# The last three units of a convolution kernel laid out in one list, with the products of points 0 and infinity of the last unit's parts ahead of the other sums

## The chip, the cores and the metric

The kernel runs on one core of one Trainium2 chip. The metric is the device time in microseconds. The core has five engines that work side by side, each on its own queue of instructions in order: PE (matmuls and transposes, results in PSUM), DVE (vector), ACT (activations and copies), POOL and SP. Transfers are issued by SP, ACT or POOL and carried out by 16 DMA engines. [...]

## The reference

A convolution of width 3 along the sequence, then a batch normalisation per output channel, then silu:

```python
B, S, C = 2, 2048, 1024        # bf16
K = 3; P = K // 2
xp = jnp.pad(x, ((0, 0), (P, P), (0, 0)))
y = sum(jnp.einsum('bsc,cd->bsd', xp[:, k:k + S, :], w[k]) for k in range(K))
inv_std = 1.0 / jnp.sqrt(var + 1e-5)
y = (y - mean) * (g * inv_std) + b
return _silu(y)
```

## The kernel before

The convolution is done in a transformed domain. Six neighbouring output rows (R = 6) come from eight products (NJ = 8), one for each of eight points: 0, plus and minus one, plus and minus two, plus and minus a half, and infinity. A batch of 2048 rows has NB = 342 such groups, the columns of all later tiles. First x is loaded in windows and transformed by small matmuls (line 258) into `T_sb`, bf16; ACT and DVE copy the results out of PSUM (lines 269 and 271). The weights of the points are formed as sums and differences, two points at a time (lines 175 and 192).

A unit is one block of 128 output channels of one batch: 8 blocks times 2 batches give 16 units. Each unit holds four PSUM banks, and the units take banks 0 to 3 and 4 to 7 in turn. A product (line 296) is eight matmuls that sum over the 1024 input channels. Products of plus and minus points share a bank: the plus product is copied out by ACT (`plus`, lines 307 and 309), the minus product is added on top, and DVE (`combine`, line 314) gets sum and difference from the two. So `minus_one` leaves a sum and a difference in the tile `sd`; `minus_two` makes the three tiles `t0`, `t1`, `t2`, each two outputs wide, from `sd` and the two low banks; `minus_half` makes from them and the two high banks the six outputs: rows 0 and 1 in the low banks, rows 4 and 5 in the high banks, rows 2 and 3 in `t1`. Only row 0 needs the product of point 0, and only row 5 that of infinity. These two are added on top of bank 0 and bank 3 last of all (`first` and `last`), and ACT applies scale, offset and silu (line 319) into `yT`: row 0 and row 5 by one instruction each, rows 1 and 4 by one, rows 2 and 3 by one.

In a unit's `run`, the finish of the unit before is woven in. A whole unit then goes out by a transposing transfer on SP (`turn`, line 427) and five stores (`store`, lines 438 and 442), on SP, or on POOL for the last three whole units.

I call the last units n, q, p and then the last one, which is worked as two parts: a, of 229 columns (SPLIT), in banks 4 to 7, and b, of 113 columns, in banks 0 to 3. The parts are turned by PE transposes instead (`flip`, line 399), copied out of PSUM by DVE (line 400) and stored in pieces (`ship`, lines 414 and 420). Lines 501 to 547 of the kernel before are a written order of calls: each call issues all its instructions at once, and so sets each engine's queue. Copies of a plus product live in `cpool`, three buffers; `dpool` and `ypool2` hold `sd` and the `t` tiles. Each part's products 0 and infinity come last on PE (lines 533, 535, 540, 542). Stores of part a: six on SP and POOL; of b: one on ACT and a small one on SP, after everything.

Of the kernel before, what the change touches and what calls it, by code (L numbers as in the profile page):

```python
# [9 lines left out]
ALU = mybir.AluOpType  # L10
FP32 = mybir.dt.float32
# [4 lines left out]
P = 128  # L16
R = 6
NJ = 8
# [4 lines left out]
XBUFS = 12  # L23
SPLIT = 229
WT = 21

@with_exitstack
def kernel(
# [10 lines left out]
    nc = tc.nc  # L39
# [3 lines left out]
    NB = -(-S // R)  # L43
    NT = B * NB
    NW = -(-NB // WT)
    LAST = NB - WT * (NW - 1)
    assert S % P == 0 and NB <= 512
# [7 lines left out]
    ypool = ctx.enter_context(tc.tile_pool(name="ypool", bufs=1))  # L55
    dpool = ctx.enter_context(tc.tile_pool(name="dpool", bufs=1))
    ypool2 = ctx.enter_context(tc.tile_pool(name="ypool2", bufs=2))
    cpool = ctx.enter_context(tc.tile_pool(name="cpool", bufs=3))
    opool = ctx.enter_context(tc.tile_pool(name="opool", bufs=2))
    xwin_scope = ExitStack()  # L60
    xpool = xwin_scope.enter_context(tc.tile_pool(name="xpool", bufs=XBUFS))
# [8 lines left out]
    rows = consts.tile([4 * DC, P], BF16, name="rows")  # L70
# [6 lines left out]
    def transform_matrix():  # L77
        v = nc.vector
        val = consts.tile([P, 3, WT], I32, name="val")
        nc.gpsimd.iota(val, pattern=[[1, 3], [-R, WT]], base=-1, channel_multiplier=1)  # L80
        m = consts.tile([P, 4, 3, WT], FP32, name="m")
        f = consts.tile([P, 3, 2, WT], FP32, name="f")
        c = consts.tile([P, 2, WT], FP32, name="c")
# [56 lines left out]
    def load_w(pair, k, half=None):  # L140
        if (pair, "tile") not in raw:
            raw[pair, "tile"] = wpools[pair % 2].tile([P, 3, CT, 2, P], BF16, name=f"wch{pair % 2}")
        wch = raw[pair, "tile"]
        h0, h1 = (0, 2) if half is None else (half, half + 1)
        cols = slice((2 * pair + h0) * P, (2 * pair + h1) * P)
        nc.sync.dma_start(  # L146
            out=wch[:, k, :, h0:h1].rearrange("p c h d -> p c (h d)"), in_=w_all[:, k, :, cols]
        )
        clock["dma"] += 1200.0 * (h1 - h0)
        for h in range(2):  # L150
            raw[2 * pair + h] = wch[:, :, :, h]
# [3 lines left out]
    def idle(work):  # L155
        if work:
            work.pop(0)()
# [122 lines left out]
    class Unit:  # L280
# [86 lines left out]
        def run(self, between, prev, finish, prepare=None):  # L367
# [19 lines left out]
            if prepare:  # L387
                idle(act_work)
                idle(dve_work)

        def flip(self, o, blocks, rows, bank, evac):
            i0, i1 = min(rows), max(rows)
            every = slice(i0, i1 + 1, 1 if i1 == i0 else (i1 - i0) // (len(rows) - 1))
            n = blocks[0][1]
            v = ps[:, bank].bitcast(BF16)[0:n, 0:len(rows) * len(blocks) * P]
            v = v.rearrange("p (i k d) -> p i k d", i=len(rows), k=len(blocks))
            for a, i in enumerate(rows):
                for q, (t, m, _) in enumerate(blocks):
                    nc.tensor.transpose(v[:, a, q], self.yT[:, i, t:t + m], ident)  # L399
            evac(o[0:n, every, blocks[0][2]:blocks[-1][2] + 1], v)  # L400

        def ship(self, o, block, lo, rows, queues):
            i0, i1 = min(rows), max(rows)
            every = slice(i0, i1 + 1, 1 if i1 == i0 else (i1 - i0) // (len(rows) - 1))
            outs = out[self.bi, :, self.dc * P:(self.dc + 1) * P]
            full = S // R
            t, m, k = block
            hi = min(t + m, full)
            cuts = [lo, lo + (hi - lo) // 16 * 16]
            if cuts[-1] < hi:  # L410
                cuts.append(hi)
            queues = list(queues)
            for c0, c1 in zip(cuts, cuts[1:]):
                queues.pop(0).dma_start(
                    out=outs[c0 * R:c1 * R].rearrange("(p i) d -> p i d", i=R)[:, every],
                    in_=o[c0 - t:c1 - t, every, k],
                )
            cut = [i for i in rows if i < S % R]
            if t + m > full and cut:
                queues.pop(0).dma_start(  # L420
                    out=outs[full * R + cut[0]:full * R + cut[-1] + 1].rearrange("(p i) d -> p i d", p=1),
                    in_=o[full - t:full - t + 1, cut[0]:cut[-1] + 1, k],
                )
# [57 lines left out]
    between = Between()  # L481
    seq = [(dc, bi) for dc in range(DC) for bi in range(B)]
    before = prev = None
    for i, (dc, bi) in enumerate(seq[:-1]):
        unit = Unit(dc, bi, i % 2 * 4)
        unit.run(between, prev, prev, 1 if i == 0 else 2 if i == 2 else dc + 2 if bi == 1 and 0 < dc < DC - 2 else None)
        if i == 0:
            while between.jobs:
                between()
            xwin_scope.close()  # L490
            olast = ctx.enter_context(tc.tile_pool(name="olast", bufs=1))
            wpools[1] = ctx.enter_context(tc.tile_pool(name="wpool1", bufs=1))
        if i in (0, 4, 8):
            for k in range(3):
                load_w(i // 4 + 1, k)
        if prev:
            prev.turn()
        if before:
            before.store([nc.gpsimd] * 5 if i == len(seq) - 2 else ())
        before, prev = prev, unit  # L500
    dc, bi = seq[-1]
    yT = olast.tile([P, R, NBP], BF16, name="yTlast")
    a, b = Unit(dc, bi, 4, 0, SPLIT, yT), Unit(dc, bi, 0, SPLIT, NB, yT)
    sp, ac, po = nc.sync, nc.scalar, nc.gpsimd
    rows = tuple(range(R))
    ablocks, bblocks = [(0, P, 0), (SPLIT - P, P, 1)], [(SPLIT, NB - SPLIT, 0)]
    free = (DC // 2) % 2
    turned = wpools[free].tile([P, 3, CT, 2, P], BF16, name=f"wch{free}").rearrange("p k c h d -> p (k c h) d")
    op, oa, ob = (
        turned[:, R * lo:R * hi].rearrange("p (i k) d -> p i k d", i=R)  # L510
        for lo, hi in ((0, NK), (NK, NK + 2), (NK + 2, NK + 3))
    )
    dve, act = nc.vector.tensor_copy, nc.scalar.copy
    a.scratch()
    b.scratch(a)
    a.plus(3, 1, between)
    a.plus(0, 3, between, 4.0)
    prev.silu_inner()
    prev.first(between)
    prev.last(between)  # L520
    a.minus_one(between)
    prev.turn(op)
    a.minus_two(between)
    before.store([po] * 5)
    prev.store([po] * 5)
    b.plus(3, 1, between)
    b.plus(0, 3, between, 4.0)
    a.plus(2, 5, between)
    b.minus_one(between)
    a.minus_half(between)  # L530
    b.minus_two(between)
    b.plus(2, 5, between)
    a.first(between)
    a.silu_inner()
    a.last(between)
    b.minus_half(between)
    a.flip(oa, ablocks, rows[1:5], 6, dve)
    a.ship(oa, ablocks[0], 0, rows[1:5], (sp,))
    a.ship(oa, ablocks[1], P, rows[1:5], (sp, po))
    b.first(between)  # L540
    b.silu_inner()
    b.last(between)
    a.flip(oa, ablocks, (0, R - 1), 5, dve)
    a.ship(oa, ablocks[0], 0, (0, R - 1), (sp,))
    a.ship(oa, ablocks[1], P, (0, R - 1), (sp, po))
    b.flip(ob, bblocks, rows, 1, dve)
    b.ship(ob, bblocks[0], SPLIT, rows, (ac, sp))

_INS = ['x', 'w', 'mean', 'var', 'g', 'b']
_OUTS = [((2, 2048, 1024), 'bfloat16')]  # L550
# [24 lines left out]
```

## Time and profile before

| what | value |
|---|---|
| median of 6 runs | 193.39 us (193.13 to 194.15) |
| profiled execution | 194.28 us |
| its span | 192.5 us |
| PE busy | 176.5 us, 92% of the span |
| DVE busy | 156.2 us, 81% |
| POOL busy | 148.5 us, 77% |
| ACT busy | 110.0 us, 57% |
| DMA | 32.30 MB, mean 168 GB/s |

The times of the runs and the profile are from different executions; the profiled one lies above the median, and its own time is 1.78 us more than its span. Start times are microseconds from the span's start. "SPq", "ACTq" and "POOL ... DMA_DIRECT2D" rows are issues of transfers, not the transfers themselves. A row of the timeline may merge several instructions ("x4"), and its brackets give the idle time of the engine before it and what ended that. A wait is put down to whatever came last.

### The profile page before, as it was taken

The numbers are of one execution on the slowest core, as the hardware profiler recorded it, in microseconds if no ns is written. First come the engines' busy times: TensorE is split into PE (matmuls) and PEld (weight loads), VectorE is DVE, ScalarE is ACT, GpSimd is POOL, SyncE is SP. The second block draws the span as 40 slices with busy tenths as digits, with TensorE's granted clock in tenths as the row PEclk, the third lists the DMA queues.
The fourth block names the chain that finished last, engine by engine and source line by source line (L and its number), as shares of the span: only waits on it lengthen the run. The fifth ranks groups of instructions, "written<-read, shape, count | busy, mean of one in ns | idle before, by whom it ended". The sixth has DMA issues, their size and how long they took to land.

```text
span 192.5 us, 3675 instructions
## 1 busy us (share of the span) xinstructions
PE 176.5 (92%) x1379; PEld 124.4 (65%) x1379; DVE 156.2 (81%) x220; ACT 110.0 (57%) x185; POOL 148.5 (77%) x93
## 2 busy tenths in 40 slices
PE   1857989999999999999999999999999999999860
PEld 1846768666666666666666666666666666678740
DVE  5668976689978799987998899879988998573860
ACT  3768886774546565465545563646283736367450
POOL 5559999906796879999999999699999780251780
PEclk9999999999999999999999999999999999999995
DMA  6999999074142837498759658959578294979973
GB/s 184 315 329 323 325 338 282 12 215 117 31 91 49 183 69 167 143 217 204 138 119 208 113 120 221 211 132 204 110 154 169 62 147 90 210 148 150 188 152 71
DMA packets 83567, 32.30 MB, mean 168 GB/s; under 512 B 69764, under 2 KB 79005, under 8 KB 83549
## 3 DMA queue, kind: packets, MB, share of 16 engines
q1 hardware_dynamic: 82012, 30.30, 69.4%
q0 software_dynamic: 784, 1.58, 3.9%
q10 hardware_dynamic: 752, 0.18, 0.5%
q8 instruction: 11, 0.18, 0.4%
q14 instruction: 8, 0.06, 0.1%
HBM read 14.82 MB, written 8.39 MB: 121 GB/s over the span
## 4 chain that ended last, share of the span: by engine, by line
PE 80%; DMA 7%; ACT 4%; SPq 3%; DVE 2%; issue 1%; ACTq 0%; DVEq 0%
PE ps L296 76%; DMA xw<-in_x_dram 4%; PE ps L258 3%; DMA xfirst<-in_x_dram 3%; ACT T_sb L269 3%; SPq L131 2%; ACT yTlast L319 2%; DVE T_sb L271 1%; SPq L146 1%; PE ps L399 1%; DVE ps L314 1%; DVE wch_2123 L400 0%; ACT pc L307 0%; ACTq L307 0%; DVEq L400 0%
## 5 line engine op out<-in xcount | busy, mean ns | idle before, releaser
L307 ACT COPY pc<-ps 128x342 f32<-128x342 f32 (+2 forms) x34 | 14.5, 427 | 33.0 <-PE ps L296 30.5
L258 PE MATMUL ps<-rm,xw 128*128 128x168 bf16 (+1 forms) x256 | 25.2, 241 | 8.0 <-DVE rm L101 3.9
L269 ACT CAST T_sb<-ps 128x672 bf16<-128x672 f32 (+1 forms) x37 | 25.6, 736 | 8.1 <-PE ps L258 7.9
L271 DVE CAST T_sb<-ps 128x672 bf16<-128x672 f32 x29 | 23.6, 855 | 7.8 <-PE ps L258 7.5
L258 PEld LDWEIGHTS <-xw 128*128 128x128 bf16 (+1 forms) x256 | 19.9, 100 | 13.2 <-DMA xw<-in_x_dram 7.6
L314 DVE SCALAR_TENSOR_TENSOR ps<-ps,pc 128x342 f32<-128x342 f32 (+2 forms) x34 | 16.9, 498 | 7.1 <-PE ps L296 5.5
L319 ACT ACTIVATE yT_142<-ps,beta,scale 128x342 bf16<-128x342 f32 (+1 forms) x24 | 17.4, 732 | 5.9 <-PE ps L296 5.9
L319 ACT ACTIVATE yT_143<-ps,beta,scale 128x342 bf16<-128x342 f32 (+1 forms) x21 | 15.4, 732 | 5.9 <-PE ps L296 5.9
L314 DVE SCALAR_TENSOR_TENSOR sd<-pc,ps 128x342 f32<-128x342 f32 (+2 forms) x17 | 8.3, 488 | 12.8 <-ACT sd L307 12.6
L438 POOL DMA_DIRECT2D out_dram<-o x8 | 6.1, 896 | 15.9 <-DMA o<-yT_142 9.2
L307 ACT COPY sd<-ps 128x342 f32<-128x342 f32 (+2 forms) x17 | 7.3, 429 | 9.9 <-PE ps L296 9.8
L309 ACT ACTIVATE pc<-ps 128x342 f32<-128x342 f32 (+2 forms) x17 | 7.5, 441 | 9.4 <-PE ps L296 6.6
L296 PE MATMUL ps<-T_sb,wch_1507 128*128 128x342 bf16 (+2 forms) x80 | 10.8, 279 | 0.5 <-DVE ps L314 0.4
L296 PE MATMUL ps<-T_sb,wch_156 128*128 128x342 bf16 x64 | 10.6, 307 | 0.0
L296 PE MATMUL ps<-T_sb,wch_678 128*128 128x342 bf16 x64 | 10.6, 307 | 0.0
L296 PE MATMUL ps<-T_sb,wch_1089 128*128 128x342 bf16 x64 | 10.6, 307 | 0.0
L296 PEld LDWEIGHTS <-wch_1507 128*128 128x128 bf16 x80 | 7.2, 97 | 3.2 <-issue 0.9
L192 POOL TENSOR_TENSOR u_668<-e_666,w1x_664 128x1024 bf16<-128x1024 f32 x2 | 4.2, 2128 | 6.5 <-DVE e_666 L175 6.5
L296 PEld LDWEIGHTS <-wch_678 128*128 128x128 bf16 x64 | 6.2, 97 | 3.1
L296 PEld LDWEIGHTS <-wch_156 128*128 128x128 bf16 x64 | 6.2, 97 | 3.1
L296 PEld LDWEIGHTS <-wch_1089 128*128 128x128 bf16 x64 | 6.2, 97 | 3.1
L296 PE MATMUL ps<-T_sb,u_292 128*128 128x342 bf16 x32 | 6.1, 308 | 0.1
(256 smaller groups left out, 494.2 us busy)
## 6 DMA issues: line engine op xcount, KB each, us to landing
xw<-in_x_dram SPq DMA_DIRECT2D x30, 256.0 KB
out_dram<-o SPq DMA_DIRECT2D x24, 192.0 KB
wch_156<-in_w_dram SPq DMA_DIRECT2D x6, 256.0 KB
wch_678<-in_w_dram SPq DMA_DIRECT2D x3, 512.0 KB
wch_1089<-in_w_dram SPq DMA_DIRECT2D x3, 512.0 KB
wch_1507<-in_w_dram SPq DMA_DIRECT2D x3, 512.0 KB
out_dram<-o SPq DMA_DIRECT2D x12, 120.0 KB
out_dram<-o POOLq DMA_DIRECT2D x4, 192.0 KB, 4.1
```

What stands on the lines that cost most here:

```text
L131: nc.sync.dma_start(out=xw[0:hi - lo, :], in_=x[bi, lo:hi, :])
L146: nc.sync.dma_start(out=wch[:, k, :, h0:h1].rearrange("p c h d -> p c (h d)"), in_=w_all[:, k, :, cols])
L192: nc.gpsimd.tensor_tensor(u[:, i], sums[dc, q], o, op=op)
L258: nc.tensor.matmul(v[:, c * nb // nct, c % (nct // nb)], lhsT=xw[0:rows, (c0 + c) * P:(c0 + c + 1) * P], rhs=rm[0:rows, :, 0:n], start=Tru ...
L269: nc.scalar.copy(dst, src)
L271: nc.vector.tensor_copy(dst, src)
L296: nc.tensor.matmul(self.bank[q], lhsT=lhsT, rhs=T_sb[:, ct, j, nsl], start=not add and ct == 0, stop=ct == CT - 1, skip_group_check=add,)
L307: nc.scalar.copy(dst, self.bank[q])
L309: nc.scalar.mul(dst, self.bank[q], by)
L314: nc.vector.scalar_tensor_tensor(out=out, in0=in0, scalar=scalar, in1=in1, op0=ALU.mult, op1=op1)
L319: nc.scalar.activation(self.yT[:, rows, self.lo:self.hi], src, ACT.Silu, bias=beta[:, dc:dc + 1], scale=scale[:, dc:dc + 1])
L438: q.dma_start(out=rows[lo * R:hi * R].rearrange("(p i) d -> p i d", i=R), in_=o[p0:p0 + hi - lo, :, k])
```

## The change

Five things change.

1. The loop over units stops one earlier, and unit p joins a and b in a list of steps, `ORDER`. A name in the list is a unit's letter (q, p, a, b) and a step: `1`, `2`, `3` the plus products, `n1`, `n2`, `n3` the minus products, a number with `c` its copy, with `d` its DVE combination, `t0` to `t2`, `y0` to `y2` the sums, `0` and `8` the products of point 0 and infinity, `s..` the silus, `T` and `S` turn and store, `f` and `S` with a number flip and ship.
2. For a and b, the product of point 0 is added on the bank of the one-points after their sum was copied out, and copied out again (`0c`); the product of infinity goes into bank 1 and is added by DVE to the difference of the one-points (`8d`). A new tile `z` holds the four values. `t0` and `t2` then read pairs of `z`, so that rows 0 and 5 have their extra products before the sums. Each part needs three silus of two rows each.
3. For q and p the arithmetic is as before; q's product of point 0 comes right after p's first product, and a's first, second and infinity products ahead of p's last two.
4. Part a is flipped in rows 4 and 5 (bank 6, copied by ACT) and rows 0 to 3 (bank 4, copied by DVE); part b in three pairs of rows, copied by DVE. Stores of a: SP, ACT and one on POOL for its last five groups; of b: both on SP.
5. `cpool` has four buffers.

```diff
+EVAC_A = [0, 1]
+SHIP_A = [[0, 0], [0, 1]]
+SHIP_B = [0, 0]
+EVAC_B = [0, 0, 0]
+ORDER = """
+p1 q0 p2 p1c pn1 qs1 p2c pn2 pn2d qs0 p3 pn1c q8 p3c pn3 pn1d nS a2 qs2 pt2 pt1 pt0 qs5 pn3d py0 py1 a1 py2
+a1c ps2 a8 ps1 p0 p8 a2c an1 qT an2 an1d b8 ps0 ps5 qS a8d b1 b1c an2d an1c a3 a0 bn1 at2 a3c an3 b3 at1 bn1d
+a0c bn1c b2 b2c at0 b3c b0 b0c an3d b8d bn2 ay0 ay1 ay2 as0 as2 bn2d bn3 bn3d bt0 as1 bt1 af1 by1 bt2 by0 pT
+bs1 bs0 by2 af0 bf0 aS1 bf1 bs2 pS aS2 aS0 bf2 bS
+"""
-    cpool = ctx.enter_context(tc.tile_pool(name="cpool", bufs=3))
+    cpool = ctx.enter_context(tc.tile_pool(name="cpool", bufs=4))
+        def steps(self, z):
+            s0, s1, d1, z5 = (z[:, q, self.lo:self.hi] for q in range(4))
+            pairs = {
+                "t0": (0, -0.0125, z[:, 0:3:2, self.lo:self.hi]), "t1": (1, -0.05, z[:, 1:3, self.lo:self.hi]),
+                "t2": (2, -0.2, z[:, 1:4:2, self.lo:self.hi]),
+            }
...
+            else:
+                f["n1c"] = lambda: self.copy(3, dst=s1)
+                f["n1d"] = lambda: self.combine(d1, self.pc[3], 2.0, self.bank[3], ALU.subtract)
+                f["0"], f["0c"] = part(3, 0, True), lambda: self.copy(3, dst=s0)
+                f["8"], f["8d"] = part(1, NJ - 1, False), lambda: self.combine(z5, self.bank[1], 1.0, d1)
+                for k, (key, (_, a, pair)) in enumerate(pairs.items()):
+                    f[key] = lambda k=k, a=a, pair=pair: self.combine(t(k), self.low, a, pair)
+                f["s0"] = lambda: self.silu(slice(0, 2), self.low)
+                f["s1"] = lambda: self.silu(slice(2, 4), self.y23)
+                f["s2"] = lambda: self.silu(slice(4, 6), self.high)
+            return f
...
-    for i, (dc, bi) in enumerate(seq[:-1]):
+    for i, (dc, bi) in enumerate(seq[:-2]):
...
+    z = olast.tile([P, 4, NB], FP32, name="z")
...
-    a.plus(3, 1, between)
-    a.plus(0, 3, between, 4.0)
-    prev.silu_inner()
-    prev.first(between)
-    prev.last(between)
...
+    steps = {}
+    for name, u in (("q", prev), ("p", p), ("a", a), ("b", b)):
+        steps.update((name + k, f) for k, f in u.steps(z).items())
+    steps["qT"] = prev.turn
+    steps["pT"] = lambda: p.turn(op)
+    steps["nS"] = lambda: before.store([po] * 5)
+    steps["qS"] = lambda: prev.store([po] * 5)
+    steps["pS"] = lambda: p.store([po] * 5)
+    queue = (sp, ac, po)
+    low, high = tuple(range(4)), (4, 5)
+    steps["af0"] = lambda: a.flip(oa, ablocks, low, 4, (dve, act)[EVAC_A[0]])
+    steps["af1"] = lambda: a.flip(oa, ablocks, high, 6, (dve, act)[EVAC_A[1]])
+    steps["aS0"] = ships_a(low, [queue[q] for q in SHIP_A[0]])
+    steps["aS1"] = ships_a(high, [queue[q] for q in SHIP_A[1]])
+    steps["aS2"] = lambda: a.ship(oa, ablocks[1], P + 96, low + high, (po,))
+    for q in range(3):
+        steps[f"bf{q}"] = flips(b, ob, bblocks, 2 * q, q, (dve, act)[EVAC_B[q]])
+    steps["bS"] = lambda: b.ship(ob, bblocks[0], SPLIT, tuple(range(R)), [queue[q] for q in SHIP_B])
+    for k in ORDER.split():
+        steps[k]()
```

More of the change, by code (lines that the diff above doesn't have):

```diff
@@ L389, in run, with old @@
                 idle(dve_work)
+        def steps(self, z):
[4 more added lines that the diff above has]
+            }
+            nop = lambda: None
+            put = lambda q, by=None: self.pc.__setitem__(q, self.copy(q, by=by))
+            part = lambda q, j, add: (lambda: self.product(q, j, add, nop))
+            t = lambda k: (self.t0, self.t1, self.t2)[k]
+            def old():
+                self.combine(self.sd[:, 1], self.pc[3], 2.0, self.bank[3], ALU.subtract)
+            late = self.hi - self.lo == NB
+            f = {
+                "1": part(3, 1, False), "1c": lambda: put(3), "2": part(0, 3, False), "2c": lambda: put(0, 4.0),
+                "n1": part(3, 2, True), "n2": part(0, 4, True), "3": part(2, 5, False), "3c": lambda: put(2),
+                "n3": part(2, 6, True),
+                "n2d": lambda: self.combine(self.bank[1], self.bank[0], -2.0, self.pc[0]),
+                "n3d": lambda: self.combine(self.bank[3], self.bank[2], -0.5, self.pc[2]),
+                "y0": lambda: self.combine(self.low, self.high, -1.6, self.t0),
+                "y1": lambda: self.combine(self.t1, self.high, -0.4, self.t1),
+                "y2": lambda: self.combine(self.high, self.high, -0.1, self.t2),
+            }
+            if late:
+                f["n1c"] = lambda: self.copy(3, dst=self.sd[:, 0])
+                f["n1d"] = old
+                for k, a in enumerate((-0.0125, -0.05, -0.2)):
+                    f[f"t{k}"] = lambda k=k, a=a: self.combine(t(k), self.low, a, self.sd)
+                f["0"], f["8"] = part(0, 0, True), part(3, NJ - 1, True)
+                f["s0"] = lambda: self.silu(0, self.bank[0])
+                f["s5"] = lambda: self.silu(R - 1, self.bank[3])
+                f["s1"] = lambda: self.silu(slice(1, 5, 3), self.mid)
+                f["s2"] = lambda: self.silu(slice(2, 4), self.y23)
+            else:
[9 more added lines that the diff above has]
+            return f
@@ L400, in flip, with ship @@
             evac(o[0:n, every, blocks[0][2]:blocks[-1][2] + 1], v)
-        def ship(self, o, block, lo, rows, queues):
+        def ship(self, o, block, lo, rows, queues, whole=False):
             i0, i1 = min(rows), max(rows)
@@ L408, in ship @@
             hi = min(t + m, full)
-            cuts = [lo, lo + (hi - lo) // 16 * 16]
-            if cuts[-1] < hi:
+            cuts = [lo, lo + (hi - lo) // 16 * 16] if hi - lo > 16 else [lo]
+            if cuts[-1] < hi and not whole:
                 cuts.append(hi)
@@ L498 @@
         if before:
-            before.store([nc.gpsimd] * 5 if i == len(seq) - 2 else ())
+            before.store()
         before, prev = prev, unit
-    dc, bi = seq[-1]
     yT = olast.tile([P, R, NBP], BF16, name="yTlast")
-    a, b = Unit(dc, bi, 4, 0, SPLIT, yT), Unit(dc, bi, 0, SPLIT, NB, yT)
+    z = olast.tile([P, 4, NB], FP32, name="z")
     sp, ac, po = nc.sync, nc.scalar, nc.gpsimd
-    rows = tuple(range(R))
-    ablocks, bblocks = [(0, P, 0), (SPLIT - P, P, 1)], [(SPLIT, NB - SPLIT, 0)]
     free = (DC // 2) % 2
@@ L512 @@
     )
-    dve, act = nc.vector.tensor_copy, nc.scalar.copy
+    ablocks, bblocks = [(0, P, 0), (SPLIT - P, P, 1)], [(SPLIT, NB - SPLIT, 0)]
+    p = Unit(*seq[-2], len(seq) % 2 * 4)
+    a, b = (Unit(*seq[-1], b0, lo, hi, yT) for b0, lo, hi in ((4, 0, SPLIT), (0, SPLIT, NB)))
+    p.scratch()
     a.scratch()
     b.scratch(a)
-    a.plus(3, 1, between)
-    a.plus(0, 3, between, 4.0)
-    prev.silu_inner()
-    prev.first(between)
-    prev.last(between)
-    a.minus_one(between)
-    prev.turn(op)
@@ L523 @@
[L523 to L547, printed above, removed]
+    def flips(u, o, blocks, i, bank, evac):
+        return lambda: u.flip(o, blocks, (i, i + 1), bank, evac)
+    def ships_a(rows, queues):
+        def go():
+            a.ship(oa, ablocks[0], 0, rows, queues[:1])
+            a.ship(oa, ablocks[1], P, rows, queues[1:2], True)
+        return go
@@ new lines @@
+    dve, act = nc.vector.tensor_copy, nc.scalar.copy
+    steps = {}
[9 more added lines that the diff above has]
+    steps["af0"] = lambda: a.flip(oa, ablocks, low, 4, (dve, act)[EVAC_A[0]])
```

## The prediction, made before the result was known

> **What bounds the kernel now.** I began with the whole-span view (PE busy 92%, DVE 81%, POOL 77%, ACT 57%), then took the chain that ended last, because shares alone do not say where the tail is set. Columns: start, duration, what.
>
> ```profile
> 40.74 137.37 PE ps L296 x968
> 178.19 0.36 ACT pc L307
> 178.59 0.96 PE ps L296 x8
> 179.57 0.42 DVE ps L314
> 180.71 0.97 PE ps L296 x8
> 181.70 1.84 ACT yTlast L319 x3
> 183.58 0.51 PE ps L399 x6
> 186.01 0.61 PE ps L399 x4
> 186.71 0.56 DVE wch_2123 L400
> ```
>
> From 40.7 to 178.1 us the matmuls run without a break, so nothing before 178 can pay unless it removes matmuls. After that PE, ACT and DVE hand the last unit to each other. The timeline of the tail gives the engines' queues (start, duration, engine, line, idle in brackets):
>
> ```profile
> 171.63 3.67 SPq L427 DMA_TRANSPOSE o<-yT_143  x1
> 175.82 2.86 SPq L427 DMA_TRANSPOSE wch_2123<-yT_142  x1
> 176.19 0.39 DVE L314 SCALAR_TENSOR_TENSOR sd<-pc,ps 128x229 f32<-128x229 f32 x1 [3.33 <-ACT sd L307]
> 182.15 2.93 POOL L438 DMA_DIRECT2D out_dram<-wch_2123  x4 [1.13 <-DMA wch_2123<-yT_142]
> 184.17 0.39 DVE L314 SCALAR_TENSOR_TENSOR ps<-ps,t_2126 128x226 f32<-128x226 f32 x1
> 185.18 2.04 SPq L414 DMA_DIRECT2D out_dram<-wch_2123  x4
> 187.30 0.69 ACTq L414 DMA_DIRECT2D out_dram<-wch_2123  x1
> ```
>
> The last matmul ends at 185.2 (start 184.02 plus 1.17), the last store is issued at 187.30, and the span ends at 192.5. The view of busy time by window says what happens in those 5.2 us (the last two columns are the DMA engines' share and GB/s):
>
> ```profile
> 188.00:188.25 0.25, 0.00 (x0) 0.00 (x0) 0.00 (x0) 0.00 (x0) 0.00 (x0) 0.50 0.92 197
> 188.50:188.75 0.25, 0.00 (x0) 0.00 (x0) 0.00 (x0) 0.00 (x0) 0.00 (x0) 0.50 0.11 22
> 189.00:189.25 0.25, 0.00 (x0) 0.00 (x0) 0.00 (x0) 0.00 (x0) 0.00 (x0) 0.50 0.88 191
> 190.50:190.75 0.25, 0.00 (x0) 0.00 (x0) 0.00 (x0) 0.00 (x0) 0.00 (x0) 0.50 0.06 12
> 190.75:191.00 0.25, 0.00 (x0) 0.00 (x0) 0.00 (x0) 0.00 (x0) 0.00 (x0) 0.50 0.00 0
> ```
>
> Part a's stores keep the DMA engines busy until 188.6; the last store (part b, 168 KB) moves from 189.0, 1.7 us after its issue, has stragglers to 190.75, and 1.75 us of closing follow. So two chains end nearly together: the compute chain to the last store's issue, and the DMA backlog of p's store (packets from 183.5), a's and b's.
>
> [...]one backlog, 85 to 100% busy from 183.5 to 188.5. [...]by 180.0 the hardware queue's bulk (both transposes) was over, yet POOL waited for p's transpose until 182.15 while q's store moved. [...]Here SP's 185.18 issue showed packets about 1.1 us later and ACT's 187.30 issue 1.7 us later[...]. The trace has 0.275 us for 113 columns and 0.40 for 229, about 0.15 fixed.
>
> **The change, step by step.** [...]Prices, all from rows after 150 us: a product holds PE 1.16, 0.79 or 0.40 us (342, 229, 113 columns), readable 1.32, 0.95, 0.57 after its start. The vector combine's starts are 0.545 us apart at 458 columns, 0.305 at 226; singles last 0.40 (229) and 0.275 (113), the next may start 0.085 earlier. ACT copies last 0.45, 0.355, 0.26 and overlap the next by 0.11; silus of 458 columns follow 0.63 to 0.66 apart, of 226 about 0.46. A hand-over costs 0.04.
>
> *Removed and added.* Per part one silu goes (0.54 or 0.44) and one ACT copy comes (0.355 or 0.26), plus one vector add (0.40 or 0.275). Matmuls and transposes are as many as before; PSUM evacuations go from 3 to 5 and part stores from 8 to 7. A fourth copy buffer only loosens ACT waits beneath the unbroken PE stretch: zero, since matmuls cover it. Before p nothing else moves.
>
> *PE.* The part products 0 and infinity leave the tail, so PE should no longer stop at 178 to 181: the same products back to back end at 182.9 instead of 185.2. That is 2.3 us won on PE. But the two infinity products now run ahead of b's first product: before, that started at 176.34; after, 176.34 + 0.79 + 0.40 - 0.09 (a's second product had waited 0.09 for q's silu, no longer) = 177.43. p's last product needs p's low and high sums from DVE; p's four-product's subtraction slips two products, its last sum comes at about 173.95 and the product at 174.29: 0.3 to spare.
>
> *Where the gain goes first.* ACT's queue has b's first copy ahead of a's copy after its minus-one product. b's product is readable at 177.43 + 0.57 = 178.00; its copy starts 178.04, a's 178.19, done 178.54. Vector's three a-sums queue behind that: they start 178.58, where they started 176.98 before. Vector is idle for nearly 1 us ahead of them.
>
> *The vector chain.* From 178.58: two sums to 179.67; b's difference waits for its product (start 179.42, readable 179.98), 180.02; third sum 180.21; a's half-difference 180.81 (product readable 180.77); b's infinity add 181.13; a's three results 181.32, 181.86, 182.41, the last readable 183.04; b's two differences 182.95, 183.14; b's six sums at 183.33, 183.64, 184.07 (a dependence), 184.37, 184.80 (another), 185.11; readable 185.50. Before it was 184.17 + 0.39 = 184.56. Vector is 0.94 later, although PE is 2.3 earlier.
>
> *The ACT chain.* a's high silu waits for 183.04: 183.08. Then a's inner silu 183.71, the copy of four transposes 184.37 (moved here from DVE; 512 columns, not shown on ACT: 0.59 by the slope of the three copies), b's silus 184.85 and 185.31, then ACT itself issues a store of a at 185.73, and the last silu is queued behind it. The issue costs 0.41 (SP's shortest such row) to 0.69 (ACT's row); at nothing, if ACT could run on, the silu starts 185.73. I take 0.5: 186.2, readable 186.75; two transposes 187.07; copy of 256 columns 0.29 (slope of the 512, 768 and 1024 rows): 187.40; last store issued 187.43. The same reckoning over the old order gives 187.08 where the trace has 187.30, so I add 0.22: 187.65, against 187.30. The compute chain is 0.35 later; with the bounds of the issue and the copy, -0.15 to +0.6.
>
> *Queues.* POOL stores q when its transpose has landed. q's transpose is issued at about 170.6 instead of 171.63 (q's last silu moved up), p's at 176.4 instead of 175.82 (p's last product is later by one part product). p's transpose lands about 0.6 later, so p's store starts near 182.75 and its packets near 184.1 instead of 183.5. POOL is queued there, with the 5-row piece of a behind it: one DMA now, so about as late as before. SP's queue holds four of a's and b's stores; the last store, now on SP, queues behind a's 224 KB. By bytes, a's packets then end at about 188.6 + 0.5 = 189.1 where before they ended 188.6 with 0.4 us idle after. b's packets start at the later of 189.1 and 187.65 + 1.1 to 1.7 = 188.75 to 189.35: about 189.3 against 189.0. The small second store behind it is hidden by the stragglers.
>
> **Sum.** +0.3 us: span 192.8. That execution took 194.28, 1.78 beyond its span and 0.89 over the median of six, 193.39; the difference is put on the median: **193.7 us**. This kernel's runs scatter by about half a percent, and 0.3% (0.58 us) is about what a measurement can tell from no change.
>
> **Rivals.** (1) Likeliest, 0.42: the chains cancel within 0.58 us as above; its own range is 192.9 to 193.95. (2) Slower by a collision, 0.22. Place: the DMA engines between 176 and 184. Before, q's store packets followed p's transpose; after, q's store is issued up to 1 us earlier and p's transpose 0.6 later, so they overlap[...]. It decides once p's transpose lands after about 183.2 (I expect 182.7): then a and b wait behind p one for one. One microsecond gives 193.7 + 0.9 = 194.6. For it: the 2.2 us between p's data and its landing before. Against: the bytes are unchanged. (3) Slower by the ACT queue, 0.16. Place: ACT from 183 to 187, where every delay moves the last silu one for one. With the issue at 0.69 and the 512-column copy at the 0.736 of the 672-column cast it is +0.3; it decides when the last silu starts after about 186.7 (0.22 included), and a further 0.3 of waits gives 194.3. For it: ACT has no idle left there in my reckoning. Against: none of its waits is on PE. (4) Faster, 0.20: ACT's issue holds nothing up (-0.45), and the last store has SP's 1.1 us delay instead of ACT's 1.7 (-0.6), provided that a's packets are gone by 188.3: the end is 0.75 earlier than my sum, 192.9, and 192.6 if the 512-column copy also hides. It decides once the last store's packets start before 188.4. For it: PE frees 2.3 us. Against: DMA share near 0.9 until 188.5. A change that never reaches the tail is excluded: the order on PE differs.
>
> **Range.** The low end holds rival 4 whole, 192.5; the high end rivals 2 and 3 with a collision of up to 1.4 us, 195.0. About 1 in 10 is left out on each side.
>
> **What would show it.** Right: matmuls unbroken to about 182.9 with the PE gap of 1 us now ahead of the first transpose; DVE idle about 0.9 us near 177.7, released by ACT; a's sums starting near 178.6; the last vector sum ending near 185.7; an ACT store issue ahead of the last silu; the last store issued near 187.65. Wrong: PE gaps before 182, p's transpose landing at or before 182.1 with the last store before 187.1 (faster), or after 183.2 with DMA still saturated at 190 (slower).

## The result

The change made the kernel slower: 196.58 us (median of 10 runs, 194.23 to 198.05) against 193.79 us (20 runs). The ratio is 1.0113, with a 95% interval of 1.0082 to 1.0145; ratios here are of fast runs alone, and two of these ten, at 197.87 and 198.05 us, count as slow, so the medians lie further apart than the ratio. I had predicted 193.7 us, within 0.3% of no change, as the likeliest, with 195.0 at the top of the range. The profiled execution took 195.84 us; its span is 194.1 us, 1.6 us more than before.

In this execution p's first product starts at 161.79 us, where it was 161.48, because the loading of x at the start took a little longer: in the chain, the load of `xfirst` ends at 20.65 us, before at 20.40, and PE's unbroken stretch starts at 41.04, before at 40.74. This offset of 0.31 us has nothing to do with the change: over the executions below, that start lies anywhere between 161.01 and 162.74 us. First the chain that ended last, of the changed kernel:

```profile
41.04 141.26 PE ps L306 x1024
182.31 0.47 PE ps L306 x7
182.78 0.56 DVE ps L324
...
186.92 0.85 POOL out_dram L495
188.28 0.56 POOL out_dram L471
```

The unbroken stretch of PE now reaches the last matmuls, so that part of the change works: PE no longer stops between 178 and 181. But the chain passes to POOL at 186.92, which it did not before. The timeline of the changed kernel shows what came late (start, duration, engine, line):

```profile
176.77 2.77 SPq L484 DMA_TRANSPOSE wch_2029<-yT_142  x1
177.09 2.95 POOL L495 DMA_DIRECT2D out_dram<-o  x4 [5.88 <-DMA o<-yT_143]
178.89 0.63 DVE L324 SCALAR_TENSOR_TENSOR t_2036<-ps,z 128x458 f32<-128x458 f32 x1 [0.71 <-ACT z L317]
184.84 2.93 POOL L495 DMA_DIRECT2D out_dram<-wch_2029  x4 [4.29 <-DMA wch_2029<-yT_142]
185.26 4.83 SPq L471 DMA_DIRECT2D out_dram<-wch_2029  x4
185.36 0.39 DVE L324 SCALAR_TENSOR_TENSOR ps<-ps,t_2036 128x226 f32<-128x226 f32 x1
185.55 0.36 ACTq L471 DMA_DIRECT2D out_dram<-wch_2029  x1
185.61 0.96 ACT L329 ACTIVATE yTlast<-ps,beta,scale 128x226 bf16<-128x226 f32 x2
186.62 0.72 DVE L457 COPY wch_2029<-ps 113x256 bf16<-113x256 bf16 x3 [0.27 <-PE ps L456]
190.13 0.64 SPq L477 DMA_DIRECT2D out_dram<-wch_2029  x1
```

The computing ends where it did: b's last copy is over at 186.62 + 0.72 = 187.34 (before 186.71 + 0.56 = 187.27), and 0.24 us earlier than before once the offset of 0.31 is taken off. The transfers are late. POOL waited until 184.84 for p's transpose, where it had been 182.15; the transpose, issued at 176.77, took 8.1 us instead of 6.3. Beside it runs q's store on POOL, issued 0.32 us after the transpose. In the kernel before it came 1.72 us after it:

```profile
177.54 2.96 POOL L438 DMA_DIRECT2D out_dram<-o  x4 [6.62 <-DMA o<-yT_143]
```

And SP's four stores (now three of a and the large one of b) stretch over 4.83 us of issues and end at 190.09, although b's data were ready at 187.34. Before, SP's four stores, all of a, took 2.04 us.

The windows of the changed kernel (last two columns: DMA share and GB/s) show a hole, then a backlog:

```profile
184.00:185.00 1.00, 0.80 (x12) 0.64 (x12) 0.97 (x3) 1.00 (x3) 0.16 (x1) 1.00 0.01 3
185.00:186.00 1.00, 0.21 (x4) 0.04 (x1) 0.97 (x4) 1.00 (x3) 1.00 (x2) 1.00 0.06 16
188.00:189.00 1.00, 0.00 (x0) 0.00 (x0) 0.00 (x0) 0.00 (x0) 0.85 (x2) 0.50 1.12 198
191.00:192.00 1.00, 0.00 (x0) 0.00 (x0) 0.00 (x0) 0.00 (x0) 0.00 (x0) 0.50 0.76 160
```

For two microseconds the DMA engines have almost nothing to do, because p's store waits for p's transpose and its packets start at 186.37, 1.53 us after its issue at 184.84; then p, a and b come together and run until 192. Between 187 and 188 us the queues of the kernel before and of the changed one differ as follows (q1 is SP's, q10 ACT's, q0 POOL's; packets, MB, share of the engines). Before:

```profile
q1 hardware_dynamic: 656, 0.16, 77.7%
q0 software_dynamic: 62, 0.01, 8.5%
```

After:

```profile
q0 software_dynamic: 40, 0.11, 59.4%
q10 hardware_dynamic: 177, 0.04, 23.6%
q1 hardware_dynamic: 14, 0.00, 1.4%
```

Before, POOL had almost finished and SP's stores of a had the engines. After, POOL's p store takes most of them and ACT's one store some, while SP's queue, in which a's large stores and b's wait, stands.

### The profile page after: what moved, and what is told of

Its sections match the earlier page's. It is cut to its first block, busy times and chain, and to the rows that moved or that the text cites. A ratio compares the mean times of both kernels' runs of the same rounds, so it can differ in the third digit from the quotient of the medians.

```text
span 194.1 us, 3662 instructions
## 1 busy us (share of the span) xinstructions
PE 176.9 (91%) x1379; PEld 125.5 (65%) x1379; DVE 156.5 (81%) x223; ACT 110.3 (57%) x186; POOL 148.0 (76%) x92
## 4 chain that ended last, share of the span: by engine, by line
PE 80%; DMA 10%; SPq 3%; ACT 2%; DVE 1%; POOL 1%; issue 0%; POOLq 0%; ACTq 0%
PE ps L306 76%; DMA xw<-in_x_dram 7%; PE ps L268 3%; DMA xfirst<-in_x_dram 3%; SPq L141 2%; ACT yTlast L329 1%; SPq L156 1%; DVE T_sb L281 0%; POOL out_dram L495 0%; ACT T_sb L279 0%; POOL out_dram L471 0%; DVE ps L324 0%; POOLq L627 0%; ACT wch_2029 L457 0%; PE ps L456 0%
## 5 line engine op out<-in xcount | busy, mean ns | idle before, releaser
L268 PE MATMUL ps<-rm,xw 128*128 128x168 bf16 (+1 forms) x256 | 26.2, 250 | 7.2 <-DVE rm L111 3.9
L268 PEld LDWEIGHTS <-xw 128*128 128x128 bf16 (+1 forms) x256 | 21.3, 105 | 12.1 <-DMA xw<-in_x_dram 6.7
L324 DVE SCALAR_TENSOR_TENSOR sd<-pc,ps 128x342 f32<-128x342 f32 x15 | 7.6, 508 | 7.2 <-ACT sd L317 7.1
L317 ACT COPY sd<-ps 128x342 f32<-128x342 f32 x15 | 6.7, 445 | 9.8 <-PE ps L306 9.8
```

The source lines that it names most:

```text
L268: nc.tensor.matmul(v[:, c * nb // nct, c % (nct // nb)], lhsT=xw[0:rows, (c0 + c) * P:(c0 + c + 1) * P], rhs=rm[0:rows, :, 0:n], start=Tru ...
L317: nc.scalar.copy(dst, self.bank[q])
L324: nc.vector.scalar_tensor_tensor(out=out, in0=in0, scalar=scalar, in1=in1, op0=ALU.mult, op1=op1)
```

## The experiments

Four theories were put against each other. A: q's store on POOL runs beside p's transpose, and this holds back the transpose's completion, and so p's store and all behind it. B, an addition to A: p's store on POOL then keeps SP's stores waiting. C: the compute chain of a and b got later. D: the transpose or POOL's queue is late by itself, one for one. Each ratio is to runs of the kernel before from the same session (its medians there: 193.96, 194.13 and 194.62 us).

**q's store on SP.** The changed kernel with one move:

```diff
-... b8 ps0 ps5 qS a8d ... bt2 by0 pT
+... b8 ps0 ps5 a8d ... bt2 by0 pT qS
-    steps["qS"] = lambda: prev.store([po] * 5)
+    steps["qS"] = lambda: prev.store([sp] * 5)
```

> The changed kernel with one move: unit q's five stores are issued by SP behind p's transpose instead of by POOL. Theory A (q's store on POOL runs beside p's transpose and holds back its last packets and its completion): p's transpose, issued near 176.8, lands before 182.5 instead of 184.8, POOL starts p's store there, the last store is issued before 188, and the time falls by 1.5 to 2.5 us, to about 193.5 to 194.5. Rival C (the compute chain of a and b is what got later): the last copy of part b ends as before near 187.3 and the time stays within 0.6 us of the changed kernel's. Rival D (p's transpose lands late only because it is issued 0.95 us later): it lands no earlier than 183.1 less 0.3, and the time stays within 1 us of the changed kernel's.

Measured: 193.86 us, ratio to the kernel before 0.9999 (0.9976 to 1.0022). The whole loss is gone, with the arithmetic and the order of the computing untouched. Timeline of this run:

```profile
177.71 2.69 SPq L484 DMA_TRANSPOSE wch<-yT  x1
180.49 2.95 SPq L495 DMA_DIRECT2D out_dram<-o  x4
...
182.56 2.94 POOL L495 DMA_DIRECT2D out_dram<-wch  x4 [10.33 <-DMA wch<-yT]
```

The transpose takes 182.56 - 177.71 = 4.85 us instead of 8.1. (This execution began 0.95 us later than the changed kernel's, so its absolute times are later.) C falls, and so does a transpose that is late by its issue alone: neither the computing nor the issue of the transpose was changed. Whether POOL's own queue is late is settled further down.

**Head as before.** Units q and p in their old order, parts a and b in the new one:

```diff
-p1 q0 p2 p1c pn1 qs1 p2c pn2 pn2d qs0 p3 pn1c q8 p3c pn3 pn1d nS a2 qs2 pt2 pt1 pt0 qs5 pn3d py0 py1 a1 py2
-a1c ps2 a8 ps1 p0 p8 a2c an1 qT an2 an1d b8 ps0 ps5 qS a8d ...
+p1 p1c p2 p2c pn1 pn1c pn1d pn2 pn2d pt0 pt1 pt2 p3 p3c qs1 qs2 q8 qs5 pn3 pn3d py0 py1 py2 q0 qs0 qT nS
+a1 a1c a2 a2c ps1 ps2 p0 ps0 p8 ps5 a8 an1 pT an2 an1d b8 qS a8d ...
-... bt2 by0 pT
+... bt2 by0
```

> The changed kernel with units q and p ordered as before the change (q's and p's products, copies and silus, and a's first two products ahead of p's last two); parts a and b as in the changed kernel. Theory A: p's transpose is issued near 175.8 again, lands near 182.1, and the time is that of the kernel before or up to 0.5 us less (193.2 to 193.9). Rival C (a's and b's new arithmetic costs the time): the time stays near that of the changed kernel, 195.5 or more.

Measured: 194.02 us, ratio 0.9996 (0.9975 to 1.0017). The transpose was issued at 175.34 and POOL went on at 182.47: it took 7.13 us, 0.8 more than in the kernel before, and still there is no loss. So the new arithmetic of a and b costs nothing that can be measured, and gains nothing: the loss sits in the head, where q and p were laid out anew.

**The kernel before, with p late.** The opposite test, with none of the new arithmetic (in this kernel `prev` is p and `before` is q; in the changed one they are q and n):

```diff
+    a.minus_one(between)
     prev.silu_inner()
     prev.first(between)
     prev.last(between)
-    a.minus_one(between)
     prev.turn(op)
```

> The kernel before with one move: part a's minus-one product, copy and difference ahead of p's silus and last two products, so that p's transpose is issued about 0.9 us later; no arithmetic is changed. Theory A: p's transpose, overlapping q's store on POOL longer, lands 2 to 3 us later than before (182.15), near 184.5, and the time rises by 1.5 to 2.5 us over the kernel before. Rival D (a late issue costs its own lateness and no more): it lands near 183.0 and the time rises by 0.3 to 0.9 us. Rival C: the time rises by less than 0.3 us, since nothing of a's and b's arithmetic is new.

Measured: 195.58 us, ratio 1.0104 (1.0073 to 1.0136), nearly the loss of the change. Timeline:

```profile
176.69 2.83 SPq L427 DMA_TRANSPOSE wch<-yT  x1
...
177.43 2.95 POOL L438 DMA_DIRECT2D out_dram<-o  x4 [6.40 <-DMA o<-yT]
184.44 2.92 POOL L438 DMA_DIRECT2D out_dram<-wch  x4 [3.56 <-DMA wch<-yT]
```

A transpose issued 0.87 us later (176.69 against 175.82) landed 2.29 us later. b's last copy ended only 0.34 us later (187.61). D's own price for a late issue, 0.3 to 0.9 us, is too small; A's holds.

**p's store on SP.** The changed kernel, with p's store behind p's transpose on SP:

```diff
-... bt2 by0 pT ... bs2 pS aS2 ...
+... bt2 by0 pT pS ... bs2 aS2 ...
-    steps["pS"] = lambda: p.store([po] * 5)
+    steps["pS"] = lambda: p.store([sp] * 5)
```

> The changed kernel with one move: unit p's five stores are issued by SP, behind p's transpose, instead of by POOL; q's store stays on POOL. Theory A with B (p's transpose still lands late, near 184.8; and p's store in large POOL packets keeps the small packets of SP's stores waiting, so that SP's issues of the last stores stretch from 0.5 to 1.7 us): the landing stays at 184.8, but SP's issues are 0.4 to 0.7 us each again; p's store then delays a's and b's on SP by its own 3.5 us of issues, and the time is within 1 us of the changed kernel's. If the starving were the main loss and the landing a minor one, the time would fall by over 1 us. Rival C: unchanged within 0.3 us.

Measured: 196.16 us (4 runs), ratio 1.0122 (1.0055 to 1.0190). p's store started at 184.79, as in the changed kernel. SP's four stores of a and b then took 2.27 us of issues, 0.42 to 0.69 each, where they had taken 4.83. So B's effect is there, but curing it in this way gains nothing: p's store, late as it is, now stands ahead of a's and b's on SP, whose issues begin at 188.93. In the runs without a loss whose stores of a and b are the changed kernel's, the four issues took 2.88 to 3.61 us, so a moderate stretch costs nothing.

**q's store last on POOL.** Behind p's store instead of ahead of it, so that no store at all moves beside p's transpose:

```diff
-... b8 ps0 ps5 qS a8d ... bs2 pS aS2 ...
+... b8 ps0 ps5 a8d ... bs2 pS qS aS2 ...
```

> The changed kernel with q's store behind p's on POOL's queue, so that no store runs beside p's transpose. Theory A: p's transpose, issued near 176.8, lands before 182 (its issue plus about 5 us) where the changed kernel had 184.84. The time gains nothing for sure, since q's 504 KB now move at the end beside a's and b's: 195 to 197. Rival D: the landing stays near 184.8, whoever stores what.

Measured: 196.0 us, ratio 1.0101 (1.0073 to 1.0128). p's store began at 181.84, 4.82 us after the transpose's issue at 177.02. The landing was cured and the time was not: now q's 512 KB (504 KB of it in the three large stores) are in POOL's queue at the end, and SP's four issues stretch to 4.55 us. In this run the early landing did not help, with q's store issued on POOL from 184.99 to 188.75, just when SP's last ones came.

**One product moved.** Part a's product of infinity behind p's two:

```diff
-a1c ps2 a8 ps1 p0 p8 a2c
+a1c ps2 ps1 p0 p8 a8 a2c
```

> The changed kernel with one product moved: part a's product of infinity behind p's products of 0 and infinity instead of ahead of them. That lets p's last silu end up to 0.8 us earlier (less if PE has to wait for p's last sum). Theory A: p's transpose is issued near 176.2 instead of 176.8, its bulk is nearly over when q's store begins to move, so it lands near 182.5 to 183.5 and the time falls by 1 to 2 us, to about 194 to 195. Rival D (the order of a's product does not matter): within 0.4 us of the changed kernel.

Measured: 194.43 us, ratio 1.0010 (0.9988 to 1.0032). The time is within what A expected; the way to it is not. Counted from p's first product, the transpose was issued as late as in the changed kernel: 177.17 - 162.19 = 14.98 us here, 176.77 - 161.79 = 14.98 there. PE now waited 0.23 us ahead of p's last product for DVE's last sum of p. So DVE's sums of p hold p back, and moving the part product alone cannot bring p forward. These sums slipped in the change: p's first combination of two banks starts 167.87 - 161.79 = 6.08 us after p's first product in the changed kernel and 166.32 - 161.48 = 4.84 before, later by about the 1.16 us of q's product that was put ahead. What differs in this execution is q: its transpose took 6.8 us to POOL's next issue instead of 6.0, so q's store began 1.24 us after p's transpose was issued, not 0.32. The packets show where q's transpose was held: of its last 32 packets 30 had started 4.50 us after its issue, and the last two started at 5.35, when a packet of 16 KB from an instruction queue, begun at 4.20, ended. In all the other executions such a packet came 1.1 to 2.1 us after q's issue. No run moved it, and one execution can't say whether the other runs of this kernel had the same lead.

**POOL delayed on purpose.** If the lead of p's transpose over q's store is what counts, useless work on POOL ahead of q's store must make the kernel faster:

```diff
+    pad = olast.tile([P, 6 * P], BF16, name="pad")
-    steps["qS"] = lambda: prev.store([po] * 5)
+    def later():
+        v = prev.o.rearrange("p i k d -> p (i k d)")
+        for _ in range(1):          # 2 in the second run
+            po.tensor_tensor(pad, v[:, 0:6 * P], v[:, 6 * P:12 * P], op=ALU.add)
+        prev.store([po] * 5)
+
+    steps["qS"] = later
```

> The changed kernel with one added useless POOL instruction (a sum of 768 columns into a scratch tile, about 1.6 us by the 2.13 us of POOL's 1024-column rows) between the landing of q's transpose and q's store; nothing else is changed. So q's store begins about 1.9 us after p's transpose is issued, instead of 0.3 us. Theory A (the lead of p's transpose over q's store decides how long it takes; the runs so far: leads of 1.7, 1.2, 1.1, 0.7, 0.3, 0.0 us took 6.3, 6.5, 7.1, 7.7, 8.1, 8.4 us): p's transpose takes about 6.3 us instead of 8.1, p's store starts about 1.7 us earlier although POOL does more, and the time falls by 1 to 2 us. Rival D (POOL's queue itself is what is late): the time rises by up to 1.6 us.

> The same with two such instructions, about 3.2 us. Theory A: p's transpose takes 5 to 6 us, since its data are over before q's store moves; but POOL's own queue (3.2 us of sums and 3.5 us of q's issues after the landing of q's transpose near 177) now ends near 183.8, and p's store waits for that: it starts 1 us earlier than in the changed kernel and later than with one instruction. Time between the two: 0.3 to 1.2 us below the changed kernel. Rival D: 2 to 3.2 us above it.

Measured: 193.95 us with one, 193.90 us with two; the ratio is 0.9976 (0.9951 to 1.0001) for both. Timeline of the first:

```profile
176.91 1.64 POOL L596 TENSOR_TENSOR pad<-o 128x768 bf16<-128x768 bf16 x1 [5.18 <-DMA o<-yT]
...
177.28 2.69 SPq L484 DMA_TRANSPOSE wch<-yT  x1
...
178.49 2.93 POOL L495 DMA_DIRECT2D out_dram<-o  x4
183.63 2.92 POOL L495 DMA_DIRECT2D out_dram<-wch  x4 [1.70 <-DMA wch<-yT]
```

With 1.64 us of useless work the loss is gone. The fall, from 1.0113 to 0.9976 of the kernel before, is more than the 1 to 2 us that A expected. D would have had it slower, so POOL's queue is not what was late. The lead came out at 1.21 us, not 1.9, because q's transpose landed earlier there, and p's transpose took 6.35 us. With two instructions the lead was 3.44 us:

```profile
180.30 2.94 POOL L495 DMA_DIRECT2D out_dram<-o  x4
183.47 3.23 POOL L495 DMA_DIRECT2D out_dram<-wch  x4
```

POOL reached p's store at 183.47 without waiting for the transpose (no bracket), and the time was no worse than with one, so the expectation that it would lie between the two was a miss on the good side.

**Both moves together.** The head as before and q's store on SP; the lines are shown against the run with the head as before:

```diff
-... an1 pT an2 an1d b8 qS a8d ...
+... an1 pT qS an2 an1d b8 a8d ...
-    steps["qS"] = lambda: prev.store([po] * 5)
+    steps["qS"] = lambda: prev.store([sp] * 5)
```

> The changed kernel with both earlier moves: units q and p ordered as before the change, and q's store on SP behind p's transpose. Parts a and b are as in the changed kernel. Theory A: p's transpose is issued near 175.3 and lands before 181, 1.5 us or more ahead of its landing with q's store on POOL; p's store is over before a's and b's start, and the last store is issued as soon as b is copied out. Time 0.5 to 1.5 us below the kernel before (192.4 to 193.4). Rival F (the end is set by b's last copy, near 187, whatever the transfers do): the time is within 0.4 us of the kernel before, as with either move alone.

Measured: 193.77 us, ratio 0.9978 (0.9955 to 1.0002). The transpose lands 4.85 us after its issue, and in the profile p's store was issued by 183.6, before a's first store at 184.6. It clearly beats the changed kernel, but it can't be told from the kernel before: the interval just takes in 1. A's gain of 0.5 to 1.5 us did not come; rival F's 0.4 us holds.

**The kernel before with q's store on SP.**

```diff
-    before.store([po] * 5)
+    before.store([sp] * 5)
     prev.store([po] * 5)
```

> The kernel before with q's five stores on SP behind p's transpose instead of on POOL; nothing else is changed. Theory A: p's transpose lands near 181 instead of 182.15 (its data were over by 180), p's store starts 1 us earlier, and the time falls by 0 to 0.6 us: the last store is issued at 187.3 as before, since b's copy sets it, and only the backlog ahead of it shrinks. Rival D: the landing stays at 182.15, the time the same.

Measured: 194.13 us, ratio 0.9988 (0.9963 to 1.0013). p's store started at 180.81 instead of 182.15, and nothing came of it. Before the change the landing was early enough, and bringing it forward gains nothing; that b's last copy then sets the end fits this, but was not tested alone.

Each row below is from one profiled execution. "Lead" is the time from the issue of p's transpose to the first issue of q's store on POOL. "Taken" runs from the issue of the transpose to the first issue of p's store, which waited for it in all but one. The packets in the traces split this time. On SP's queue the transpose is 2304 packets of 256 bytes, its data, and then 32 of 4 bytes, which I take for its completion: in the runs where both can be read, POOL's next step came 0.7 to 1.1 us after the last of these. The table gives the start of the last packet of each kind after the issue. Where q's store follows on SP, its packets can't be told from the transpose's.

| kernel | lead, us | last data packet | last 4-byte packet | taken, us |
|---|---|---|---|---|
| p's store on SP | 0.0 | 6.56 | 7.46 | 8.38 |
| changed | 0.32 | 5.58 | 7.10 | 8.07 |
| before, p late | 0.74 | 4.50 | 6.82 | 7.75 |
| head as before | 1.15 | 4.19 | 6.20 | 7.13 |
| one POOL instruction | 1.21 | 4.13 | 5.42 | 6.35 |
| one product moved | 1.24 | 4.11 | 5.38 | 6.46 |
| before | 1.72 | 4.09 | 5.40 | 6.33 |
| two POOL instructions | 3.44 | 4.07 | 4.09 | POOL did not wait |
| q's store last | - | 4.06 | 4.08 | 4.82 |
| q's store on SP (changed, both moves, before) | - | | | 4.85, 4.85, 4.92 |

Without a POOL store beside it the transpose takes 4.8 to 4.9 us. Beside one it takes up to 3.5 us more, and broadly the more the less its lead. With a lead of 1.15 to 1.72 us the data are hardly held up (4.09 to 4.19 against 4.06), but the 4-byte packets are: q's store has begun to move by then, 4.1 us after the transpose's issue. With a shorter lead the data are held up too. With 3.44 us, where q's store begins to move at 4.84, neither is. It isn't a matter of bytes: q's store has the same 512 KB in all of them. Nor is it the instruction queues: none of their packets fell between the issue of p's transpose and its landing, but for one in the run with p's store on SP, 0.07 us before the end.

How late is too late? On the clock of the kernel before (p's first product at 161.48), p's store started at 182.8 to 183.1 us with the head as before, with one product moved and with one or two POOL instructions, and none of these four shows a loss. It started at 184.3 to 184.8 in the changed kernel, with p late and with p's store on SP, and all three do.

## Why the prediction was wrong

The step that failed is the paragraph on the queues: "p's transpose lands about 0.6 later, so p's store starts near 182.75". I priced a later issue one for one. The issue was as predicted (176.4 plus the offset of 0.31 is 176.71; it was 176.77), but the landing came at 184.84 instead of 182.75 + 0.31 = 183.06, 1.8 us later than the step says. The transpose took 8.07 us where the step gave it 182.75 - 176.4 = 6.35, about what it was before. The step missed that a lead of 1.7 us had shielded the transpose in the kernel before, and that the change cut it from both sides: q's store earlier, p's transpose later.

Rival 2 named this collision and its place, and its rule (a landing after 183.2 costs one for one) gives, for 184.84 - 0.31 = 184.53, 193.7 + 1.3 = 195.0. That is 1.6 us over the 193.39 it started from; the measured rise of 1.13% is 2.2 us. Its edge at 183.2 fits the runs: no loss up to 183.1, a loss from 184.3. I gave it 0.22. The evidence that it deserved more was quoted as its support: 2.2 us between the end of p's data and its landing, in an execution where q's store began to move just as they ended. There, with a lead of 1.72 us, the last 4-byte packet started 5.40 us after the transpose's issue; with the lead of 0.32 in the changed kernel it started 7.10 us after it.

A second term was mis-sized, in the same direction. I put the packets of b's store at the later of its readiness and the end of a's bytes, about 189.3, and gave the issues of a's stores ahead of it on SP no delay of their own. SP's issues took up to 1.69 us, that of b's store began at 188.4, 1.06 us after b's data were ready at 187.34, and its 672 packets, the last large lot on SP's queue, came from about 191.0. The backlog before was also read too high: its DMA share was not 85 to 100% from 183.5 to 188.5, but 0.76 from 184 to 185 us and 0.49 from 186.0 to 186.5. The run with p's store on SP shows issues of 0.42 to 0.69 us again for the same four stores once POOL's large store is gone.

The compute steps held. With the offset of 0.31: a's sums start at 178.89 (reckoned 178.58 + 0.31), with DVE 0.71 us idle behind ACT ahead of them (reckoned nearly 1); the last vector sum is readable at 185.75 (reckoned 185.81, and 0.22 on top of it); PE's matmuls end at 182.71 + 0.56 = 183.27 (reckoned 183.2). The cost of ACT's own issue was wrong, at 0.5 us: ACT's two last silus follow each other without a gap (0.96 us for two, of which one alone is 0.53), and the issue of 0.36 us ran beside the first of them. That is most of why the computing ended 0.24 us earlier than before and not 0.35 later: 0.5 of the 0.59 us. Rival 3 (ACT) is refuted by it. Rival 4 needed ACT's issue to be free, which it was, and the last store's packets before 188.4, which was far off.

The place of the gain was right: PE's 2.3 us went into waits of DVE and ACT. What the run with both moves shows is that nothing measurable of it reaches the end even when p's transpose is undisturbed.

## What to carry to other kernels

A transfer that something waits for is priced by what runs beside it, not by its issue alone: here the same transpose took 4.8 to 8.4 us to the next step on POOL. When a change moves its issue, compare its lead over the next large transfer before and after, and see what shielded it. In a tail, put the stores that nobody waits for behind the transfer that somebody waits for; here either handing q's store to the same queue or delaying it by one or two POOL instructions removed the whole loss. Delaying it to the very end did not: SP's four issues then stretched to 4.55 us, against 2.88 to 3.61 in the runs without a loss and with the same stores.

## What the runs showed of the hardware

A transposing transfer of 576 KB (2304 packets of 256 bytes) took 4.8 to 4.9 us from its issue on SP to the next step on POOL when no POOL store ran beside it, and up to 8.4 us with a 512 KB store beside it. With a lead of 1.15 to 1.72 us, what the store behind it held up was hardly its data (last packet 4.09 to 4.19 us after the issue, against 4.06 with q's store last) but the 32 packets of 4 bytes after them (the last at 5.38 to 6.20, against 4.08). Between 187 and 188 us of the changed kernel, 40 packets of POOL's carried 0.11 MB and 14 of SP's less than 0.01 MB, while 177 of ACT's came through with 0.04 MB. Why SP's queue stood and ACT's did not, and with it the inner cause of the transpose's delay, was not shown; no run here changed the size of the packets alone. What the runs show is that taking POOL's store away from the transpose (4.85 us instead of 8.07), or p's store from POOL (2.27 us of SP's issues instead of 4.83), removes the two effects one by one.

SP's issue of a store is not a fixed price: the same four stores took 0.42 to 0.69 us each with no POOL store beside them, and up to 1.69 us while POOL's store moved. And one POOL instruction that did nothing useful for 1.64 us brought the changed kernel from 1.0113 of the time before to 0.9976.
